# Gate and up projections of a gated mix as two by two blocks with seven products

## The chip, the cores and the metric

The kernel runs on one core of a Trainium2 chip. The metric is the device time of one execution in microseconds (us); the median of several runs is given.

## What is computed

With x of 2048 × 512, 32 heads of 16 and a hidden size F of 1792, the reference is

```
g = sigmoid((x * gate_w).sum(-1))
a = softmax_attention(x @ wqkv, 32 heads) @ wo
b = (sigmoid(x @ w_gate) * (x @ w_up)) @ w_down
out = g * a + (1 - g) * b
```

Every operand of a product is kept as a high and a low part, and a product is three matmuls: high by high, high by low, low by high.

## The kernel before

The order of the instructions on PE, ACT, DVE and POOL is the order in which the program emits them. SP only issues transfers; the framework orders those, and each waits at SP until its source is ready or its target is free, with all later ones behind it.

The work has three stages. First come q and k of the first 128 rows of weights and V for all tokens. Then 256 attention steps (the loop over k, NPER). Then the down projection in 28 chunks of 24 matmuls, with the heads' output projection between them.

A step handles two blocks of S (scores) for the row maxima, and two blocks of transposed S for the exponentials. The string STEADY is a step's order on PE: eight matmuls "m" (L257), each followed by a DVE reduction (L259) that reads the bank; eight matmuls "t" (L380), each followed by an exponential on ACT (L382); twelve half matmuls "d" (L145), of 64 rows each, of a dense sum into the bank dn; and a "turn" between d1, which uses the upper rows of PE, and d0, which uses the lower. The number behind m or t is the bank. A turn (L156) is a token on POOL: an empty instruction that waits for the last half before it and that the first half behind it waits for, so it also stands behind whatever POOL has to do ahead of it. After the step's order come 16 matmuls of exponentials by V, called values (L489), into the bank sm0 (SUMS = 0); they are copied out by ACT (L494) and summed on POOL (L506).

Dense sums are runs that the generator filling hands out: q and k of the remaining weights, then gate and up, one tile of 128 columns by 512 tokens each, 24 halves a run, so two steps. When a run is done, its bank is copied out (leave, L319, by ACT; by DVE, L308, in the last ten steps) and stored to gu_d or split for q_d and k_d. Work for POOL waits in the list later and is emitted by work(n), one piece at mid-step behind the turn, two at the end of a step. The maxima run LEAD = 20 blocks ahead, so the last ten steps (k = 246 on) have none: their banks come in turn from all seven others and DVE copies. The last eight steps (TAIL) follow the shorter order LAST with six d:

```
LAST = "t0 d1 t0 d1 t0 d1 turn t0 t1 t1 d0 t1 d0 t1 d0"
```

Dense work that is left then, ten runs, is done as whole matmuls of 128 rows (L582). Beside these runs ACT and DVE prepare the first chunks of the down stage: hidden (sigmoid on ACT, L453, product on DVE, L454) and hidden_split (copy to the high part on ACT, L94, subtraction on DVE, L97). The sigmoid isn't in ACT's table for exponentials, so ACT loads another table first. The down matmuls are L673.

Of the kernel before, what the change touches and what calls it, by code (L numbers as in the profile page):

```python
# [24 lines left out]
P = 128  # L25
KT = D // P
# [12 lines left out]
TAIL = 8  # L39
# [4 lines left out]
def gated_mix(ctx, tc, x, xT, wqk, wv, wo, w_gate, w_up, w_down, gate_w, out):  # L44
# [26 lines left out]
    rec_d = dram.tile([P, 512], F32, name="rec_d")  # L71
    max_d = dram.tile([2 * NPAIR, 4, 32, 2, 32], F32, name="max_d")
# [44 lines left out]
    def split_later(h, l, src, then=None):  # L117
# [4 lines left out]
        later.append(lambda: pool.tensor_copy(h, src))  # L122
        later.append(low)
# [37 lines left out]
    later = []  # L161

    def work(n):
        while later and n:
            later.pop(0)()
            n -= 1
# [11 lines left out]
    def load_x(c, raw=None, ks=range(KT)):  # L178
        raw = raw or mid(f"x{c}")
        cols = slice(c * 512, (c + 1) * 512)  # L180
        for k in ks:
            sp.dma_start(raw[:, k, :], xT[k * P:(k + 1) * P, cols])
# [85 lines left out]
    def put_max(half):  # L268
# [15 lines left out]
        return [lambda: pool.tensor_copy(hl[:, 0, :], mt), low]  # L284
# [3 lines left out]

    def filling():
        jobs = [("qk", c) for c in range(1, D // P)] + [("gu", f) for f in range(NF)] + [("down", 0)]  # L290

        def raws(kind, n):
            if kind == "qk":
                return [raw_cols(wqk, n, f"q{n}"), raw_cols(wqk, KT + n, f"k{n}")]
            if kind == "gu":
                return [raw_cols(w_gate, n, f"g{n}"), raw_cols(w_up, n, f"u{n}")]
            return [raw_weights(w_down[f * P:(f + 1) * P, :], [P, D], f"wd{f}") for f in range(2)]

        nxt = [split_weights(r) for r in raws(*jobs[0])]
        yield None  # L300
        for j, (kind, n) in enumerate(jobs[:-1]):
            ws, nxt = nxt, []
            for c in range(NC):
                for i, w in enumerate(ws):
                    run = Sum(bankd(), unit(w, c))
                    yield run
                    e = keep.tile([P, 512], F32, name=f"{kind}{n}_{c}_{i}", tag="er", bufs=4)
                    leave(e, run.o)  # L308
                    if kind == "qk":
                        put_qk(e, (q_d, k_d)[i], n, c)  # L310
                    else:
                        sp.dma_start(gu_d[i, n, :, c * 512:(c + 1) * 512], e)
                    if (c, i) == (0, 0):
                        coming = raws(*jobs[j + 1])
# [76 lines left out]
    for t in range(2, NS, 2):  # L391
        two = [Sum(bankv(), tokens(t + a)) for a in range(2)]
        for g in (LOW, UP):
# [13 lines left out]
            if t >= 12:  # L407
                work(1)
# [307 lines left out]
```

## Time and profile before

| | us |
|---|---|
| median of 3 runs | 1733.11 (1732.87 to 1733.24) |
| the profiled execution | 1733.32 |
| its span, first to last instruction | 1731.5 |
| values of step 0 to values of step 245 | 91.04 to 1459.92 |
| the last ten steps | 1459.92 to 1502.25 |
| the ten whole runs | 1502.25 to 1531.58 |
| the down stage | 1531.58 to 1731.5 |

Times in the profile count from the first instruction of the profiled execution; its own time is 1.82 us longer than its span. The granted clock of TensorE is 1.00 throughout. A line such as L489 is the line of the kernel before, and a shape such as 128x512 is partitions by elements. Rows of a timeline give start, length, engine, line, operation, output and input; the bracket at the end is the time for which the engine stood idle just before, and what ended that.

### The profile page before, as it was taken

To read this page: it belongs to the slowest core of one execution; us is meant where nothing else is said; L and a number is where in the kernel's file an instruction comes from. 1 tells how busy PE (TensorE), PEld (TensorE's weight loads), DVE (VectorE), ACT (ScalarE), POOL (GpSimd) and SP (SyncE) were. 2 spreads that over 40 slices of the span, in tenths; PEclk is the share of its full clock that TensorE was granted. 3 is DMA by queue.
4 is the path that set the end of the run, shared out by engine and by line. 5 is a ranking of instruction groups with operands and counts; after the bars stand their busy time and mean duration, and the time that the engine had idled before them with its cause. 6 is when DMAs were issued, how large, how long until landed. Compare 5 with 4: busy or idle time off the path is not lost.

```text
span 1731.5 us, 33713 instructions
## 1 busy us (share of the span) xinstructions
PE 1724.6 (100%) x12666; PEld 1066.3 (62%) x12666; DVE 1426.1 (82%) x2291; ACT 1319.3 (76%) x2555; POOL 471.0 (27%) x437
## 2 busy tenths in 40 slices
PE   9999999999999999999999999999999999999999
PEld 7755555555555555555555555555555555588887
DVE  6988888888999999998888888888888887457543
ACT  4188888888888888888888888888888888844321
POOL 1034343432222322222222222222222222343110
PEclk9999999999999999999999999999999999999999
DMA  9312424241314131314131313131221212377752
GB/s 252 80 43 68 83 68 93 69 107 43 81 57 81 57 81 40 82 50 87 38 75 39 75 39 64 44 63 51 53 57 46 56 55 69 118 233 257 237 194 73
DMA packets 85347, 149.78 MB, mean 86 GB/s; under 512 B 18816, under 2 KB 27008, under 8 KB 82304
## 3 DMA queue, kind: packets, MB, share of 16 engines
q1 hardware_dynamic: 85184, 147.63, 31.8%
q8 instruction: 99, 1.62, 0.4%
q14 instruction: 64, 0.52, 0.1%
HBM read 87.56 MB, written 60.03 MB: 85 GB/s over the span
## 4 chain that ended last, share of the span: by engine, by line
PE 97%; DVE 2%; DMA 0%; ACT 0%; issue 0%; SPq 0%; DVEq 0%
PE dn L145 29%; PE sm L489 27%; PE sm L257 12%; PE sm L673 7%; PE st L380 7%; PE sm L380 5%; PE st L132 3%; PE st L257 2%; DVE stat L259 2%; PE dn L673 2%; PE st L346 1%; PE sm L582 1%; PE st L582 1%; PE st L145 1%; PE st L489 0%; DMA x<-in_xT_dram 0%
## 5 line engine op out<-in xcount | busy, mean ns | idle before, releaser
L259 DVE TENSOR_REDUCE stat<-sm 128x1 f32<-128x512 f32 x1310 | 848.9, 684 | 154.8 <-PE sm L380 138.0
L382 ACT ACTIVATE p<-st 128x512 f32<-128x512 f32 x1019 | 612.8, 654 | 2.3 <-PE st L380 2.3
L382 ACT ACTIVATE p<-sm 128x512 f32<-128x512 f32 x1027 | 604.8, 630 | 2.4 <-PE sm L380 1.8
L257 PE MATMUL sm<-ks,qs 48*128 48x512 f32 x1310 | 521.0, 436 | 0.2
L506 POOL TENSOR_TENSOR sum<-sum,part 128x512 f32<-128x512 f32 x224 | 289.8, 1294 | 844.5 <-PE sm L380 779.1
L489 PE MATMUL sm<-p,v 128*17 128x512 f32 x4048 | 483.8, 595 | 0.0
L259 DVE TENSOR_REDUCE stat<-st 128x1 f32<-128x512 f32 x738 | 482.6, 682 | 0.1
L380 PE MATMUL sm<-qs,ks 64*128 64x512 f32 x1027 | 426.9, 421 | 0.8 <-ACT part L494 0.8
L380 PE MATMUL st<-qs,ks 64*128 64x512 f32 x1019 | 423.3, 419 | 0.0
L257 PEld LDWEIGHTS sm<-ks,qs 48*128 48x128 f32 x1310 | 238.0, 184 | 293.7 <-DVE stat L259 212.5
L257 PE MATMUL st<-ks,qs 48*128 48x512 f32 x738 | 291.4, 395 | 0.0
L494 ACT ACTIVATE part<-sm 128x512 f32<-128x512 f32 x215 | 128.7, 599 | 170.8 <-issue 146.9
L489 PEld LDWEIGHTS sm<-p,v 128*17 128x17 f32 x4048 | 93.7, 96 | 227.0 <-issue 159.3
L380 PEld LDWEIGHTS st<-qs,ks 64*128 64x128 f32 x1019 | 186.8, 184 | 28.7 <-issue 3.4
L380 PEld LDWEIGHTS sm<-qs,ks 64*128 64x128 f32 x1027 | 188.7, 185 | 12.7 <-issue 4.3
L257 PEld LDWEIGHTS st<-ks,qs 48*128 48x128 f32 x738 | 137.7, 187 | 1.1 <-ACT v L363 0.3
L454 DVE TENSOR_TENSOR gul<-gul 128x1024 f32<-128x1024 f32 (+1 forms) x30 | 47.2, 1579 | 33.8 <-ACT gul L453 31.1
L319 ACT ACTIVATE gu<-dn 128x512 f32<-128x512 f32 x99 | 68.8, 695 | 0.0
L673 PE MATMUL sm<-wd_h,hl 128*128 128x512 f32 x208 | 67.0, 389 | 0.0
L94 ACT ACTIVATE hl<-gul 128x1024 fp32r<-128x1024 f32 (+1 forms) x30 | 29.9, 998 | 41.4 <-PE sm L673 28.8
L94 ACT ACTIVATE oh<-ot 128x1024 fp32r<-128x1024 f32 x8 | 8.5, 1061 | 55.2 <-DVE ot L631 55.2
L97 POOL TENSOR_TENSOR ol<-ot,oh 128x1024 fp32r<-128x1024 f32 x8 | 19.3, 2410 | 109.5 <-ACT oh L94 99.1
(465 smaller groups left out, 2925.0 us busy)
## 6 DMA issues: line engine op xcount, KB each, us to landing
gu_d<-gu SPq DMA_DIRECT2D x112, 256.0 KB
gul<-gu_d SPq DMA_DIRECT2D x56, 512.0 KB
qs<-q_d SPq DMA_DIRECT2D x90, 128.0 KB
ks<-k_d SPq DMA_DIRECT2D x90, 128.0 KB
pv_d<-sum SPq DMA_DIRECT2D x32, 256.0 KB
q_d<-qe SPq DMA_DIRECT2D x12, 512.0 KB
k_d<-qe SPq DMA_DIRECT2D x12, 512.0 KB
x<-in_xT_dram SPq DMA_DIRECT2D x16, 256.0 KB
```

The source lines that it names most:

```text
L132: pe.matmul(o, a, b, start=(i == 0), stop=(i == len(ops) - 1))
L145: mm = pe.matmul(self.o, a[rows], b[rows], start=(self.n == 0), stop=(self.n == 2 * len(self.ops) - 1))
L257: pe.matmul(t, qs[r:r + KM, qt * P:(qt + 1) * P], ks[r:r + KM, g * 512:(g + 1) * 512], start=True, stop=True)
L259: dve.tensor_reduce(stat[half][:, b, qt % 8, g:g + 1], t, axis=AX.X, op=ALU.max)
L319: leave = lambda e, o: act.activation(e, o, AF.Copy)
L380: pe.matmul(o, ks[r:r + KR, (kt + a) * P:(kt + a + 1) * P], qs[r:r + KR, q0:q0 + 512], start=True, stop=True)
L382: act.activation(pt[:, 2 * a + c, :], o, AF.Exp, scale=DH ** -0.5)
L454: dve.tensor_tensor(gu[:, 1, a], gu[:, 0, a], gu[:, 1, a], ALU.mult)
L489: pe.matmul(o[32 * c:32 * c + VW, :], v[:, 2 * k % 16 + a, h * VW:(h + 1) * VW], pts[c // 2][:, 2 * a + c % 2, :], start=(a == 0), stop=(a ...
L494: act.activation(e, o, AF.Copy)
L506: pool.tensor_tensor(s, s, e, ALU.add)
L673: pe.matmul(down[t], a, b, start=(f == 0 and m == 0), stop=(f == NF - 2 and m == 5))
```

## The change

Gate and up are computed as two by two blocks: x in four blocks (tokens by half of the inner size), the weights in four blocks (half of the inner size by tile f or f + 7), and seven block products with sums of blocks in place of eight. The runs get a fourth of the old inner work each, 12 halves, so one step each, and come in three kinds of jobs: "far" (7 jobs of 4 runs, products without any sums of x), "side" (14 of 4) and "chain" (14 of 8).

The sums of blocks of x are made on POOL by mix_x after each of the first four far jobs (steps 52, 56, 60, 64), from blocks of x that are loaded again; one of them replaces a part of xh and xl at once, the others are split, stored to t_d and loaded into xh and xl later by mixed_x. The sums of weights are made on POOL too (op in weights). The products are added on POOL by plus, with earlier sums loaded back from gu_d, and stored. xT is laid out by the host in blocks of 128 × 512.

The lists of deferred work have costs now: work(1.3) at mid-step and work(2.6) at the end take pieces until their costs are used up, from later first and from slow (the mixes) after it; flush takes all.

All dense work lies in attention. Steps 0 to 238 are STEADY, 239 to 245 are BARE (no dense work, the free bank dn used as an eighth), 246 to 255 LAST. The ten whole runs are gone, and the down stage follows on attention at once. The first two chunks' sigmoids become hidden_early, emitted after the values of steps 250 and 252: exponential of −x on ACT, then on DVE plus one, a reciprocal of 128 × 1024 and the product; their splits are on DVE altogether. The values of step 255 and the second split stand inside chunk 0. The logits of g are spread over steps 78 to 125.

In the kernel after, L311 is the mix's subtraction, L127 and L124 are the two operations of split_later, L324 and L330 those of put_mix, L409 is the copy out of dn by DVE, L638 to L640 are hidden_early's, L681 is DVE's copy of the values, L266, L558 and L674 are S, transposed S and values on PE, and L150 is a dense half.

On POOL around step 56 the program before has the sums of values (part51 is that of step 51), the maxima's two small operations and a weight's split:

```order
L506 TENSOR_TENSOR sum3_0_4098<-sum3_0_4098,part50_4221 128x512
L506 TENSOR_TENSOR sum3_0_4098<-sum3_0_4098,part51_4282 128x512
L506 TENSOR_TENSOR sum3_0_4098<-sum3_0_4098,part52_4341 128x512
L284 CAST mhl3_1_4397<-mt3_1_4388 128x32
L275 TENSOR_TENSOR mhl3_1_4397<-mt3_1_4388,mhl3_1_4397 128x32
L506 TENSOR_TENSOR sum3_0_4098<-sum3_0_4098,part53_4413 128x512
L506 TENSOR_TENSOR sum3_0_4098<-sum3_0_4098,part54_4473 128x512
L122 CAST g1h_4526<-g1r_4150 128x512
```

In the program after, the end of the first mix (ml1_00 to ml2_00) and the start of the second (mix0_01) stand there:

```order
L324 CAST mh1_00_4512<-mix0_00_4287 128x512
L691 TENSOR_TENSOR sum3_0_4113<-sum3_0_4113,part54_4523 128x512
L330 TENSOR_TENSOR ml1_00_4576<-mix0_00_4287,mh1_00_4512 128x512
L324 CAST mh2_00_4579<-mix1_00_4288 128x512
L330 TENSOR_TENSOR ml2_00_4582<-mix1_00_4288,mh2_00_4579 128x512
L311 TENSOR_TENSOR mix0_01_4585<-mix0_01_4585 128x512
L127 CAST xh_106<-mix0_01_4585 128x512
L124 TENSOR_TENSOR xl_107<-mix0_01_4585,xh_106 128x512
L691 TENSOR_TENSOR sum3_0_4113<-sum3_0_4113,part55_4606 128x512
```

The subtraction of the second mix has come between the low half of the mix before and the sum of values of step 55, and each reads a tile that SP has to load.

On PE, this is a STEADY step before, from the fifth m, which is the second one of the step into sm0, to the last (qs1 and ks1 are the rows of the last pair of heads):

```order
L257 MATMUL sm0_69<-ks1_101,qs1_100 128x512
L380 MATMUL st0_65<-qs1_100,ks1_101 128x512
L257 MATMUL st1_66<-ks1_101,qs1_100 128x512
L145 MATMUL dn_68<-xh_105,g12h_15646 128x512
L145 MATMUL dn_68<-xl_106,g12h_15646 128x512
L380 MATMUL sm1_70<-qs1_100,ks1_101 128x512
L380 MATMUL st2_67<-qs1_100,ks1_101 128x512
L145 MATMUL dn_68<-xh_105,g12l_15647 128x512
L257 MATMUL sm2_71<-ks1_101,qs1_100 128x512
L145 MATMUL dn_68<-xh_105,g12h_15646 128x512
L257 MATMUL sm3_72<-ks1_101,qs1_100 128x512
L145 MATMUL dn_68<-xl_106,g12h_15646 128x512
```

And this is a BARE step after, from the first m into sm0 to the values of step 239:

```order
L266 MATMUL sm0_69<-ks1_102,qs1_101 128x512
L558 MATMUL st0_65<-qs0_99,ks0_100 128x512
L266 MATMUL dn_68<-ks1_102,qs1_101 128x512
L558 MATMUL st1_66<-qs1_101,ks1_102 128x512
L266 MATMUL sm2_71<-ks1_102,qs1_101 128x512
L558 MATMUL sm1_70<-qs1_101,ks1_102 128x512
L266 MATMUL sm0_69<-ks1_102,qs1_101 128x512
L558 MATMUL st2_67<-qs1_101,ks1_102 128x512
L266 MATMUL sm3_72<-ks1_102,qs1_101 128x512
L558 MATMUL st0_65<-qs1_101,ks1_102 128x512
L674 MATMUL sm0_69<-p239_1_17029,v_98 17x512 x2
```

The second m into sm0 was followed by three others in its step; it is now followed by one, and no dense half stands between.

On DVE, the copies of the last steps before are these (part250 is of step 250; den belongs to the heads):

```order
L496 COPY part250_16742<-sm2_71 128x512
L308 COPY gu12_2_0_16770<-dn_68 128x512
L496 COPY part251_16781<-st0_65 128x512
L465 RECIPROCAL den_93<-den_93 64x512
L496 COPY part252_16821<-st2_67 128x512
L496 COPY part253_16858<-sm1_70 128x512
L496 COPY part254_16895<-sm3_72 128x512
L308 COPY gu12_2_1_16914<-dn_68 128x512
```

After, they are:

```order
L681 COPY part249_17561<-st1_66 128x512
L681 COPY part250_17600<-st2_67 128x512
L638 TENSOR_SCALAR gul0_0_17519<-gul0_0_17519 128x1024
L639 RECIPROCAL gul0_0_17519<-gul0_0_17519 128x1024
L640 TENSOR_TENSOR gul0_0_17519<-gul0_0_17519 128x1024
L409 COPY chain16_11_17632<-dn_68 128x512
L681 COPY part251_17644<-sm3_72 128x512
L650 RECIPROCAL den_94<-den_94 64x512
L681 COPY part252_17687<-sm0_69 128x512
L638 TENSOR_SCALAR gul0_2_17522<-gul0_2_17522 128x1024
L639 RECIPROCAL gul0_2_17522<-gul0_2_17522 128x1024
L640 TENSOR_TENSOR gul0_2_17522<-gul0_2_17522 128x1024
```

The reciprocals of gul0_0 and gul0_2 and the operations beside them have come between the copy of a step's values and the next copy out of dn.

The diff, cut to its core:

```diff
-TAIL = 8
+FULL = 239
+FREE = NPER - LEAD // 2
+HF = NF // 2
...
-    later = []
-    def work(n):
-        while later and n:
-            later.pop(0)()
-            n -= 1
+    later, slow, soon = [], [], []
+    def work(length):
+        while length > 0.3 and (later or slow):
+            cost, step = (later or slow).pop(0)
+            step()
+            length -= cost
...
+    def mix_x(c, k):
+        one, two = [keep.tile([P, 2, 512], F32, name=f"mix{i}_{c}{k}", tag="ev", bufs=2) for i in range(2)]
+        for to, (ci, ki) in ((one[:, 0], (c + 2, k)), (one[:, 1], (c, k)), (two[:, 0], (c + 2, k + 2)), (two[:, 1], (c, k + 2))):
+            sp.dma_start(to, xT[ci, ki])
+        def minus(to, u, w):
+            slow.append((1.3, lambda: pool.tensor_tensor(to, u, w, ALU.subtract)))
+        minus(one[:, 1], one[:, 0], one[:, 1])
+        cols = slice((c + 2) * 512, (c + 3) * 512)
+        split_later(xh[:, k, cols], xl[:, k, cols], one[:, 1], queue=slow)
+        minus(one[:, 0], two[:, 0], one[:, 0])
+        minus(two[:, 0], two[:, 0], one[:, 1])
+        minus(two[:, 1], two[:, 1], two[:, 0])
+        for n, t in enumerate((two[:, 0], one[:, 0], two[:, 1])):
+            put_mix(n, c, k, t)
...
+        def low():
+            h = out.pop((n, c, k))
+            l = keep.tile([P, 512], F32R, name=f"ml{n}_{c}{k}", tag="er", bufs=4)
+            pool.tensor_tensor(l, t, h.bitcast(F32), ALU.subtract)
+            sp.dma_start(t_d[n, 1, c, k], l.bitcast(F32))
+        out = {}
+        slow.extend([(0.65, high), (1.3, low)])
...
+        pairs = [(m, i) for i in range(HF) for m in range(2)]
+        jobs = ([("qk", n) for n in range(1, D // P)] + [("far", i) for i in range(HF)]
+                + [("side", n) for n in pairs] + [("chain", n) for n in pairs] + [("down", 0)])
...
+            elif kind == "far":
+                for m in range(2):
+                    for c in range(2):
+                        run = Sum(bankd(), quarter(ws[m], 2, c))
+                        yield run
+                        sp.dma_start(place(m, n, c), out_of(run, f"far{m}{n}_{c}"))
+            elif kind == "side":
+                m, i = n
+                for c in range(2):
+                    for a in range(2):
+                        run = Sum(bankd(), quarter(ws[a], 2 * a, c + 2))
+                        yield run
+                        if n == pairs[-1]:
+                            mixed_x(1 + a, c, 2 * a, c + 2)
+                        e = out_of(run, f"side{m}{i}_{c}{a}")
+                        if a == 0:
+                            first = e
+                            sp.dma_start(place(m, i + HF, c + 2), e)
+                        else:
+                            plus(e, e, first, place(m, i, c + 2))
+            else:
+                m, i = n
+                for c in range(2):
+                    to = [place(m, i, c), place(m, i, c + 2), place(m, i + HF, c + 2), place(m, i + HF, c)]
+                    for a, (k0, cx) in enumerate(((0, c), (2, c), (0, c + 2), (2, c + 2))):
+                        if a in (0, 2):
+                            part = keep.tile([P, 2, 512], F32, name=f"had{m}{i}_{c}{a}", tag="ev", bufs=2)
+                        had = part[:, a % 2]
+                        if a < 3:
+                            sp.dma_start(had, to[a])
+                        run = Sum(bankd(), quarter(ws[a], k0, cx))
+                        yield run
+                        e = out_of(run, f"chain{m}{i}_{c}{a}")
+                        if a in (1, 2):
+                            plus(e, e, first)
+                        if a < 3:
+                            plus(had, e, had, to[a])
+                        else:
+                            plus(e, e, first, to[a])
+                        first = e
+        def plus(to, u, w, then=None):
+            def add():
+                pool.tensor_tensor(to, u, w, ALU.add)
+                if then is not None:
+                    sp.dma_start(then, to)
+            soon.append((1.3, add))
...
+            while end in later:
+                later.pop(0)[1]()
+            ws = new
+            if kind == "far" and n < 4:
+                flush(slow)
+                mix_x(n // 2, n % 2)
+            if kind == "far" and n == HF - 1:
+                flush(slow)
+                for c in range(2):
+                    mixed_x(0, c, 2, c)
...
+    eight = seven + [dn]
+    bank7 = turns([seven[b] for b in (5, 1, 6, 2, 3, 4, 0)])
...
+    def hidden_early(m):
+        gu = loaded[m]
+        act.activation(gu[:, 0], gu[:, 0], AF.Exp, scale=-1.0)
+        dve.tensor_scalar(gu[:, 0], gu[:, 0], 1.0, 3e38, op0=ALU.add, op1=ALU.min)
+        dve.reciprocal(gu[:, 0], gu[:, 0])
+        dve.tensor_tensor(gu[:, 1], gu[:, 0], gu[:, 1], ALU.mult)
+    def hidden_split(m, engine=act):
         hl = mid(f"hl{m}", F32R).rearrange("p (a f) s -> p a f s", a=2)
-        for a in (slice(0, 1), slice(1, 2)) if m < 2 else (slice(0, 2),):
-            split(hl[:, 0, a], hl[:, 1, a], loaded[m][:, 1, a], act, dve)
+        split(hl[:, 0], hl[:, 1], loaded[m][:, 1], engine, dve)
...
+    BARE = ("m1:7 t0:5 m1:2 t0:1 m1:3 t0:6 m1:0 t0:4 "
+            "m0:7 t1:5 m0:2 t1:1 m0:0 t1:6 m0:3 t1:4")
...
-        emit(STEADY if k < NPER - TAIL else LAST, **parts)
-        if k == NPER - 1:
-            bankd = bank
-        if run.done():
-            run = next(fill)
-        else:
+        emit(STEADY if k < FULL else BARE if k < FREE else LAST, **parts)
+        if run and run.done():
+            run = next(fill, None)
+        elif run and run.n:
...
-        work(2)
+        work(2.6)
+        later.extend(soon)
+        soon.clear()
...
+        if k in (NPER - 6, NPER - 4):
+            hidden_early((k - NPER + 6) // 2)
+    flush(later)
+    bank = turns(banks)
+    hidden_split(0, dve)
     act.activation(g1, logit, AF.Sigmoid)
     dve.tensor_scalar(g0, g1, -1.0, 1.0, op0=ALU.mult, op1=ALU.add)
-    values(NPER - 1)
-    work(len(later))
-    run = whole_run(run)
-    hidden(1)
-    hidden_split(1)
-    while run:
-        run = whole_run(run)
-        work(len(later))
...
+            if (n, t) == (0, 1):
+                values(NPER - 1)
+                flush(later)
+                hidden_split(1, dve)
```

More of the change, by code (lines that the diff above doesn't have):

```diff
@@ L294, in raws @@
                 return [raw_cols(wqk, n, f"q{n}"), raw_cols(wqk, KT + n, f"k{n}")]
[L295 to L299, printed above, removed]
-        yield None
[L301 to L310, printed above, removed]
-                    else:
-                        sp.dma_start(gu_d[i, n, :, c * 512:(c + 1) * 512], e)
-                    if (c, i) == (0, 0):
-                        coming = raws(*jobs[j + 1])
-                    if (c, i) in ((1, 1), (2, 1)):
-                        nxt.append(split_weights(coming[c - 1]))
@@ L317, in filling @@
-        wd.extend(nxt)
+            if kind == "far":
+                both = []
+                for m in range(2):
+                    raw = keep.tile([P, KT, P], F32, name=f"far{m}{n}r", tag="wr", bufs=2)
+                    sp.dma_start(raw[:, 2:], gu_w[m][n][:, 2:])
+                    both.append(raw)
+                return both
+            if kind == "down":
+                return [raw_weights(w_down[f * P:(f + 1) * P, :], [P, D], f"wd{f}") for f in range(2)]
+            m, i = n
@@ L502, in values @@
             put(e)
[L503 removed]
+            later.append((1.3, lambda s=sums[half]: add(s, e)))
         def add(s, e):
```

140 lines of the change are left out of this document (107 added, 33 removed).

## The prediction

> **What bounds the kernel now.** I read the page first: its span, its engines and the chain that ended last.
> ```profile
> span 1731.5 us, 33713 instructions
> PE 1724.6 (100%) x12666; PEld 1066.3 (62%) x12666; DVE 1426.1 (82%) x2291; ACT 1319.3 (76%) x2555; POOL 471.0 (27%) x437
> PE 97%; DVE 2%; DMA 0%; ACT 0%; issue 0%; SPq 0%; DVEq 0%
> ```
> PE looks like the bound everywhere. Its "busy" counts overlapping records, so a stretch needs its own look. The windows give busy time by stage (columns: PE, PEld, DVE, ACT, POOL, clock, DMA share, GB/s).
> ```profile
> 91.04:979.53 888.49, 888.49 (x6999) 513.91 (x6997) 793.32 (x1345) 757.03 (x1511) 270.90 (x267) 1.00 0.27 66
> 979.53:1459.92 480.39, 480.39 (x3786) 278.25 (x3785) 423.67 (x709) 409.51 (x818) 119.88 (x115) 1.00 0.24 58
> 1459.92:1502.25 42.33, 41.56 (x311) 19.11 (x309) 12.94 (x17) 38.78 (x80) 13.42 (x13) 1.00 0.12 40
> 1502.25:1531.58 29.33, 29.33 (x136) 22.86 (x137) 9.07 (x11) 12.18 (x21) 9.02 (x8) 1.00 0.76 255
> 1531.58:1570.00 38.42, 38.42 (x170) 31.51 (x169) 29.07 (x16) 22.88 (x25) 22.67 (x9) 1.00 0.82 277
> ```
> The edges are starts of values matmuls, so the first two windows hold 159 and 86 steps of the attention loop: 888.49/159 = 5.59 and 480.39/86 = 5.59 us a step, although POOL works 30% of the one and 25% of the other, and only every second step ends a dense sum. Something that is the same in all of them sets the pace. Then come the last ten steps, without row maxima (42.33), the ten whole dense runs (29.33) and the start of the down stage. One step, from values(244) to values(245), in the timelines of PE and, below it, of DVE:
> ```profile
> 1454.35 1.91 PE L489 MATMUL sm<-p,v 128*17 128x512 f32 x16
> 1456.19 0.49 PE L257 MATMUL sm<-ks,qs 48*128 48x512 f32 x1
> 1458.27 0.42 PE L145 MATMUL dn<-xh,g12h 64*128 64x512 f32 x1
> 1459.92 0.62 PE L489 MATMUL sm<-p,v 128*17 128x512 f32 x4
> 1456.72 0.69 DVE L259 TENSOR_REDUCE stat<-sm 128x1 f32<-128x512 f32 x1 [0.71 <-PE sm L380]
> 1457.33 1.28 DVE L259 TENSOR_REDUCE stat<-st 128x1 f32<-128x512 f32 x2
> 1458.53 1.28 DVE L259 TENSOR_REDUCE stat<-sm 128x1 f32<-128x512 f32 x2
> ```
> Maxima follow each other by 0.60 us (1456.72, 1457.33, ... 1458.53). The fifth, the second on bank sm0, ends at 1459.81, and 0.11 later the values matmuls enter sm0. So the step is a loop through DVE: 1.84 (values to the first S matmul, 1456.19) + 0.53 (to its reduction) + 4 × 0.60 (four more in turn) + 0.69 (the fifth's length) + 0.11 = 5.57. DVE is idle 0.71 a step, but only because the first S stands behind the values. Dense matmuls ride along in this loop. **Removing dense work inside attention therefore gains nothing there**; it gains what it empties behind attention. The other condition in the loop is d0: after the mid-step token it starts 3.92 after the values (1458.27), so POOL has until then to reach the token.
>
> **Part by part.** The profiled execution is 1733.32 (span + 1.82), 0.21 above the median of 1733.11; I add to 1733.32.
>
> *Fewer products.* 112 runs of 24 halves and the 24 of q/k become 24 of q/k and 196 of 12: 2928 dense halves, not 3264. Steps 0 to 238 stay STEADY at 5.59: 0 us. A run of 12 ends in every step, so ACT copies dn out in each, not in one of two: 0.35 us more a step on average for an ACT that is busy 409.51 of 480.39, 0.82 short of full: hidden, and steps with such a copy are no longer today. POOL gets 196 adds of products, up to two a step, their operands loaded a step ahead by SP. Rows with POOL's prices:
> ```profile
> L506 POOL TENSOR_TENSOR sum<-sum,part 128x512 f32<-128x512 f32 x139 | 179.5, 1291 | 478.7 <-PE sm L380 445.7 <-DMA pv_d<-sum 19.7 <-DMA gu_d<-gu 9.9
> L122 POOL CAST qe<-qk 128x512 fp32r<-128x512 f32 x24 | 14.6, 610 | 69.1 <-ACT qk L319 55.0 <-DMA ks<-k_d 7.4 <-PE sm L380 6.7
> ```
> A chain step has up to two adds (2.6), a share of the weights (three 128x256 operations, half of 1.29 each, and two splits of 0.61 + 1.29: 5.7 for 8 steps, 0.7) and the values sum (1.3): 4.6 of 5.59, hidden with 1.0 to spare. If that cover were gone, 112 steps would pay. The blocked xT, the logits' new steps and the reloads of the mixed x change no wait that I can find: 0 to −1 for the shorter first loads, left out.
>
> *Mixing x.* After far jobs 0 to 3 (steps 52, 56, 60, 64) POOL's first instruction is a subtraction of x blocks, put ahead of the mid-step token, and SP has the loads behind the store of that very step's leave. POOL's sequencer waits for them, the token behind it, d0 for the token, and PE's S and S^T behind d0. Step 60's loads stand ahead of that store, so three of four wait. The rows that price it:
> ```profile
> 1102.32 0.62 PE L489 MATMUL sm<-p,v 128*17 128x512 f32 x4
> 1103.81 0.32 SPq L312 DMA_DIRECT2D gu_d<-gu  x1
> 1105.20 0.32 SPq L277 DMA_DIRECT2D max_d<-mhl  x1
> 1106.65 2.78 SPq L281 DMA_DIRECT2D qs<-max_d  x4
> L421 SPq DMA_DIRECT2D gul<-gu_d x56: 359/430/856, 1424.7 to 1690.6; - x56
> ```
> A leave's store issues 1.49 after the values (1103.81 − 1102.32). The two loads that the subtraction needs follow at 0.43 each: issued by 2.4. A 32 KB transfer is waited on 1.45 after its issue (1105.20 to 1106.65), and 256 KB at 255 GB/s adds 1.0 (estimate): landing near 5.0. Then the subtraction 1.29, the CAST 0.61 and the dispatch of a third one: token at about 7.3 where 3.9 was due, 3.3 lost in step 52. In steps 56 and 64 the loads also await the tiles of the mix before, whose last two low halves and a CAST (2 × 1.29 + 0.61 = 3.2) POOL does at that same place: landing 7.4, token 9.5, 5.6 each. That is 14.5; some of it may issue earlier, and I take **+13**. Bounds: 0 (nothing waits) and 18 (all four).
>
> *Steps 239 to 245, BARE.* No dense work and eight banks, but values still go into sm0, and the second S in sm0 is now the seventh of eight, not the fifth. The loop is 1.84 + 0.53 + 6 × 0.60 + 0.69 + 0.11 = 6.76, seven times 1.18 more: **+8.3**. The other end is DVE alone, 8 × 0.60 = 4.78: −5.6. I take the first, since the order of PE fixes it.
>
> *Steps 246 to 255.* Maxima are over; steps 248 to 253 took (1498.26 − 1474.97)/6 = 3.88.
> ```profile
> 1474.97 0.62 PE L489 MATMUL st<-p,v 128*17 128x512 f32 x4
> 1498.26 2.00 PE L489 MATMUL sm<-p,v 128*17 128x512 f32 x16
> 1500.40 0.69 DVE L496 COPY part<-sm 128x512 f32<-128x512 f32 x1 [3.23 <-PE sm L489]
> L465 DVE RECIPROCAL den<-den x2: 3332/3340/3349, 1489.3 to 1587.3; 64x512 f32<-64x512 f32 x2
> L453 ACT ACTIVATE gul<-gul x30: 618/1046/1064, 1507.1 to 1697.9; 128x1024 f32<-128x1024 f32 x26, 128x512 f32<-128x512 f32 x4
> L454 DVE TENSOR_TENSOR gul<-gul x30: 686/1219/3421, 1507.8 to 1700.7; 128x1024 f32<-128x1024 f32 x26, 128x512 f32<-128x512 f32 x4
> ```
> All ten would take 39, not 42.33; two exponentials (1.05, as L453) on ACT, which paces these steps, make 41. A reciprocal of 512 columns takes 3.34, so 1024 take 6.7 (a row of 64 or of 128 partitions alike, I assume). After values(250) DVE copies its part at +2.1 (as 1500.40), then scalar op (1.1, between one and two 0.69 copies), reciprocal 6.7, product 1.2; only then, at 11.8, the leave of dn, 0.69. PE's first d1 of step 252 needs that bank: due at 3.88 + 1.84 + 1.05 = 6.8, it starts at 12.5 or later: 6 lost, and ACT starves behind PE. The second, two steps on, has den's reciprocal (3.34) ahead of it and loses 6 to 7. 41 + 13 = 54.3: **+12.0**. Bounds: −1 (hidden), +15.
>
> The Trainium skill ("VectorE: DVE Perf Modes", on SBUF-only operands) says that a scalar operation on fp32 from SBUF to SBUF reads two elements a clock, where one of two tensors can't; the scalar op would then take about 0.7 and both waits would shrink by 0.4. No row of this trace has one that large.
>
> *The tail.* Before, 29.4 of whole runs cover the first hidden blocks:
> ```profile
> 1502.18 0.51 PE L582 MATMUL sm<-xh,g12h 128*128 128x512 f32 x1
> 1505.84 1.28 ACT L453 ACT_TABLE_LOAD   x1
> 1531.58 0.39 PE L673 MATMUL sm<-wd0h,hl 128*128 128x512 f32 x1
> L97 DVE TENSOR_TENSOR hl<-gul,hl x30: 689/1218/3419, 1509.2 to 1712.3; 128x1024 fp32r<-128x1024 f32 x26, 128x512 fp32r<-128x512 f32 x4
> ```
> 170 matmuls took 38.42: 0.226 each, 5.4 a chunk of 24. Chunk 1 ended 29.3 + 10.8 = 40.2 after the last dense matmul. Now: leave 0.7, hl0's CAST up to 1.4 and subtraction 1.2, chunk 0 5.4 with values(255) 1.84 inside: 10.5. Chunk 1 needs hl1, whose CAST and subtraction stand on DVE behind the product of gul0_4; that tile's two loads of 512 KB wait for the last S^T: 0.43 + 1.45 + 2.06 (at 255 GB/s), about 4 and, the second behind it, 6 to 7. The table load (1.28) and the sigmoid hide in that; product 1.2, or 3.4 beside POOL, the copy of values(255) 0.7, CAST and subtraction 1.9 to 2.6: chunk 1 starts at 10.7 to 13.1 and ends at 16.1 to 18.5. That is 24.1 to 21.7 less: **−22.9**. Later chunks had DVE and the loads about at PE's pace, and get the same: 0.
>
> Sum: 13 + 8.3 + 12.0 − 22.9 = +10.4, 1743.7; rounded **1743.5 us**.
>
> **Rivals.**
> (a) *POOL's waits in the mixes are hidden*: SP's loads are issued early, as step 60's are. 1743.7 − 13 = 1730.7. For: POOL is idle 70%. Against: the store ahead of the loads waits for ACT.
> (b) *DVE's work finds its gaps*: BARE at 4.78 (−13.9) or the reciprocals hidden (−12), beside (a): 1730.7 − 13.9 = 1717, 1705 with both. This ends faster. The three stalls sum to 33.3 against a gain of 22.9, so it decides once over 10.4 of them are hidden. For: DVE is busy only 12.94 of 42.33 there. Against: both come from the order of one queue, not from its load.
> (c) *The clock.* All windows show 1.00, none with an idle PE. If stalls of 5.6 to 6.5 dropped it, four of them would each be followed by 3.4 us at half pace: 4 × 1.7 = 7, 1750. Beside it: the Trainium skill ("TensorE: Matmul & The Clock Gate", Part 1) says that an idle window of about 3.4 us halves the clock until as long a busy one; by that rule this happens, and no row here shows it.
> (d) *POOL becomes the bound of the chain*: at 4.6 of 5.59 a late token of 0.2 in 112 steps gives +22, 1766. Against: the token is not last in POOL's step.
> (e) The change doesn't do what it says: the halves are counted in the built program, so under 1%.
>
> **How the numbers follow.** Forecast 0.50 (its own range 1737 to 1753); (a) 0.16; (b) 0.21; (c) 0.07; (d) and like 0.06. About 0.2%, 3.5 us, is what a measurement of this kernel can tell from no change: 1729.6 to 1736.6. Faster: (b) and 0.07 of (a), 0.28. Within: 0.09 of (a) and 0.03 of the forecast, 0.12. Slower: 0.60. The range leaves out half of (b) and (d): 1714 to 1756.
>
> **What would show it.** Right: waits of PE for POOL's token in steps 52, 56 and 64 only, of 3 and 5 to 6 us; BARE steps at 6.7; in steps 252 and 254 PE idle behind a DVE leave; the first down matmul 3 to 4 us after the last dense one, the second chunk's 11 to 13 after. Wrong: BARE under 5.6, no reciprocal ahead of a leave, or steps in the chain over 5.6, which would put POOL in the loop.

## The result and the profile after

| | before | after |
|---|---|---|
| median, us | 1732.99 (4 runs) | 1783.18 (4 runs, 1778.36 to 1784.94) |
| ratio | | 1.0286, 95% interval 1.0273 to 1.0298 |
| span of the profiled execution | 1731.5 | 1783.2 |

The forecast was slower, and it is slower, but by 50 us and not by 10. The page of the kernel after, with the row of the granted clock in 40 slices and the chain:

```profile
span 1783.2 us, 34285 instructions
PE 1721.3 (97%) x12450; PEld 1040.4 (58%) x12450; DVE 1434.0 (80%) x2295; ACT 1357.2 (76%) x2631; POOL 873.2 (49%) x849
PEclk9999999999899999999999999999999997899999
PE 88%; DVE 3%; DMA 3%; ACT 1%; issue 1%; POOL 1%; SPq 1%; POOLq 0%; DVEq 0%; ACTq 0%
```

PE has 216 matmuls fewer and is busy 3 us less, in a span that is 52 us longer: it now waits. Before, the chain was PE for 97%; now DVE, DMA, ACT, POOL and SP are on it. And the clock row isn't all nines any more.

The windows, first of the kernel after, then of the one before, with the same edges in the work: the values of steps 51, 70, 238, 245 and 254, the first matmul of the third chunk, the end. (Columns: length; PE, PEld, DVE, ACT, POOL; clock; DMA share; GB/s.)

```profile
375.54:506.65 131.11, 115.75 (x838) 64.50 (x836) 94.15 (x159) 95.83 (x191) 83.50 (x91) 0.91 0.51 158
506.65:1446.39 939.74, 939.74 (x7394) 542.85 (x7392) 837.91 (x1419) 841.72 (x1681) 577.22 (x571) 1.00 0.43 120
1446.39:1499.00 52.61, 40.63 (x226) 13.67 (x224) 35.24 (x59) 33.81 (x66) 14.91 (x13) 0.84 0.23 71
1499.00:1553.57 54.57, 42.08 (x270) 18.25 (x271) 29.46 (x22) 37.02 (x74) 17.10 (x15) 0.81 0.11 35
1553.57:1577.17 23.60, 20.40 (x92) 12.18 (x91) 13.67 (x11) 11.24 (x18) 14.35 (x9) 0.85 0.67 216
1577.17:1783.16 205.99, 189.52 (x817) 154.81 (x815) 100.79 (x90) 61.18 (x62) 37.32 (x14) 0.96 0.59 192
```

```profile
375.86:481.87 106.01, 106.01 (x839) 61.41 (x837) 95.16 (x163) 90.69 (x182) 27.02 (x27) 1.00 0.27 67
481.87:1420.86 938.99, 938.99 (x7395) 543.25 (x7393) 836.80 (x1415) 800.11 (x1597) 240.02 (x233) 1.00 0.24 59
1420.86:1459.92 39.06, 39.06 (x310) 22.72 (x309) 34.12 (x57) 33.06 (x67) 7.74 (x6) 1.00 0.25 82
1459.92:1498.26 38.34, 37.57 (x284) 17.45 (x282) 12.25 (x16) 34.79 (x71) 12.06 (x12) 1.00 0.13 44
1498.26:1542.76 44.50, 44.50 (x212) 33.46 (x211) 18.36 (x17) 24.94 (x41) 19.13 (x14) 1.00 0.64 211
1542.76:1731.55 188.79, 185.12 (x817) 153.02 (x815) 106.48 (x89) 60.32 (x60) 36.54 (x14) 1.00 0.60 198
```

Row by row the difference is +25.1 (the mixes), +0.8 (168 steps with seven products), +13.6 (BARE), +16.2 (last steps), −20.9 (tail) and +17.2 (the rest of the down stage); with −0.3 ahead of them that is the 51.6. Every row but the second has a clock below 1.00 after, and all had 1.00 before. What PE waited for in the whole run (us in total, number of waits, longest):

```profile
PE dn L150 <- POOLq L161: 15.4, 3, 6.0
PE dn L150 <- DVE chain L409: 11.9, 2, 6.2
PE dn L850 <- DVE hl L100: 10.6, 2, 9.6
PE sm L674 <- DVE stat L268: 6.8, 7, 1.1
PE sm L266 <- DVE stat L268: 4.8, 7, 0.7
```

Five lines: the token behind the mixes, the copy of dn behind the reciprocals, one hidden block of the down stage, and the two of BARE. Together they are 49.5. That this is near 51.6 is chance: the tail also gained 20.9, so far more was lost than these waits.

One of the mixes, in step 52, in timelines of SP, POOL and PE. The values of step 51 start at 375.54:

```profile
377.01 0.32 SPq L428 DMA_DIRECT2D gu_d<-far  x1
377.38 1.87 SPq L308 DMA_DIRECT2D mix<-in_xT_dram  x4
381.78 1.26 POOL L311 TENSOR_TENSOR mix<-mix 128x512 f32<-128x512 f32 x1 [6.53 <-DMA mix<-in_xT_dram]
383.83 0.79 PE L150 MATMUL dn<-xh,far01h 64*128 64x512 f32 x1 [3.83 <-POOLq L161]
```

The store issues 1.47 behind the values, the four loads right behind it, POOL waits for them until 6.24, and PE stands idle for 3.83 ahead of its first d0.

The first reciprocal, DVE and then PE, with two pairs of dense matmuls, one right behind the stall and one later:

```profile
1525.06 6.55 DVE L639 RECIPROCAL gul<-gul 128x1024 f32<-128x1024 f32 x1
1532.79 0.68 DVE L409 COPY chain<-dn 128x512 f32<-128x512 f32 x1
1533.52 0.79 PE L150 MATMUL dn<-xh,ca(1, 6)h 64*128 64x512 f32 x1 [6.21 <-DVE chain L409]
1534.12 0.62 PE L150 MATMUL dn<-xl,ca(1, 6)h 64*128 64x512 f32 x1
1534.54 0.62 PE L150 MATMUL dn<-xh,ca(1, 6)l 64*128 64x512 f32 x1
1540.54 0.39 PE L150 MATMUL dn<-xl,ca(1, 6)h 64*128 64x512 f32 x1
1540.78 0.39 PE L150 MATMUL dn<-xh,ca(1, 6)l 64*128 64x512 f32 x1
```

The stall is where the prediction put it. But behind it two matmuls follow each other by 0.42 us, where 0.24 us is usual. The granted clock there is 0.50, from 1529.70 to 1539.94.

The long wait of the down stage, with SP's issue of the second denominators' load after and, last, before:

```profile
1639.60 0.73 SPq L649 DMA_DIRECT2D den<-pv_d  x1
1647.21 3.35 DVE L650 RECIPROCAL den<-den 64x512 f32<-64x512 f32 x1 [15.11 <-DMA den<-pv_d]
1653.01 1.22 PE L850 MATMUL dn<-wd_h,hl 128*128 128x512 f32 x2 [9.57 <-DVE hl L100]
```

```profile
1519.28 0.47 SPq L464 DMA_DIRECT2D den<-pv_d  x1
```

Before, this load went out 12 us ahead of the down stage. After, it goes out 81 us into it, and DVE, whose order is fixed, stands still for it with the next hidden block behind. Its source, the last sum of values, was stored at 1513.05 before and is stored at 1570.94 after, since values(255) now stand in chunk 0; so 69 of the 81 us are the place in SP's queue.

### The profile page after: what moved, and what is told of

It is laid out like the page before. It is cut to its first block, busy times and chain, and to the rows that moved or that the text cites. A ratio compares the mean times of both kernels' runs of the same rounds, so it can differ in the third digit from the quotient of the medians.

```text
span 1783.2 us, 34285 instructions
## 1 busy us (share of the span) xinstructions
PE 1721.3 (97%) x12450; PEld 1040.4 (58%) x12450; DVE 1434.0 (80%) x2295; ACT 1357.2 (76%) x2631; POOL 873.2 (49%) x849
## 4 chain that ended last, share of the span: by engine, by line
PE 88%; DVE 3%; DMA 3%; ACT 1%; issue 1%; POOL 1%; SPq 1%; POOLq 0%; DVEq 0%; ACTq 0%
PE dn L150 27%; PE sm L674 26%; PE sm L266 12%; PE st L558 6%; PE sm L850 4%; PE sm L558 4%; PE st L266 2%; PE st L137 2%; DVE stat L268 2%; PE st L150 1%; PE dn L850 1%; DMA gul<-gu_d 1%; PE st L524 1%; ACT p L560 1%; DVE gul L639 1%
## 5 line engine op out<-in xcount | busy, mean ns | idle before, releaser
L560 ACT ACTIVATE p<-st 128x512 f32<-128x512 f32 x1034 | 620.7, 645 | 4.0 <-PE st L558 3.7
L266 PE MATMUL sm<-ks,qs 48*128 48x512 f32 x1317 | 524.8, 439 | 5.3 <-DVE stat L268 4.8
L674 PE MATMUL sm<-p,v 128*17 128x512 f32 x4032 | 494.2, 608 | 6.8 <-DVE stat L268 6.8
L268 DVE TENSOR_REDUCE stat<-st 128x1 f32<-128x512 f32 x717 | 467.7, 680 | 0.2 <-PE st L266 0.2
L558 PE MATMUL st<-qs,ks 64*128 64x512 f32 x1034 | 436.3, 425 | 0.0
L558 PE MATMUL sm<-qs,ks 64*128 64x512 f32 x1012 | 426.7, 424 | 0.6 <-ACT p L560 0.6
L266 PEld LDWEIGHTS sm<-ks,qs 48*128 48x128 f32 x1317 | 240.5, 185 | 298.9 <-DVE stat L268 215.9
L266 PE MATMUL st<-ks,qs 48*128 48x512 f32 x717 | 283.1, 395 | 0.0
L674 PEld LDWEIGHTS sm<-p,v 128*17 128x17 f32 x4032 | 94.5, 98 | 242.6 <-issue 163.4
L558 PEld LDWEIGHTS st<-qs,ks 64*128 64x128 f32 x1034 | 192.4, 187 | 30.9 <-issue 5.7
L558 PEld LDWEIGHTS sm<-qs,ks 64*128 64x128 f32 x1012 | 188.2, 187 | 11.4 <-issue 4.3
L466 POOL TENSOR_TENSOR had<-chain,had 128x512 f32<-128x512 f32 x84 | 108.0, 1285 | 64.3 <-PE sm L558 36.1
L266 PEld LDWEIGHTS st<-ks,qs 48*128 48x128 f32 x717 | 133.8, 187 | 1.4 <-ACT v L541 0.3
L466 POOL TENSOR_TENSOR chain<-chain,chain 128x512 f32<-128x512 f32 x84 | 108.6, 1293 | 23.0 <-PE st L558 11.7
L466 POOL TENSOR_TENSOR side<-side,side 128x512 f32<-128x512 f32 x28 | 36.2, 1291 | 79.6 <-PE sm L558 74.2
L497 ACT ACTIVATE chain<-dn 128x512 f32<-128x512 f32 x107 | 73.7, 689 | 0.0
```

The costliest lines, as they stand in the source:

```text
L266: pe.matmul(t, qs[r:r + KM, qt * P:(qt + 1) * P], ks[r:r + KM, g * 512:(g + 1) * 512], start=True, stop=True)
L268: dve.tensor_reduce(stat[half][:, b, qt % 8, g:g + 1], t, axis=AX.X, op=ALU.max)
L466: pool.tensor_tensor(to, u, w, ALU.add)
L497: leave = lambda e, o: act.activation(e, o, AF.Copy)
L558: pe.matmul(o, ks[r:r + KR, (kt + a) * P:(kt + a + 1) * P], qs[r:r + KR, q0:q0 + 512], start=True, stop=True)
L560: act.activation(pt[:, 2 * a + c, :], o, AF.Exp, scale=DH ** -0.5)
```

## The experiments

The theory after the result: (A) each stall stands where the trace names it, and (B) a stalled or partly idle PE loses its clock and pays a second time. The rivals are named run by run; the stages are those of the windows above.

### The mixes' work, later

```diff
+    wait = [0]
     def work(length):
-        while length > 0.3 and (later or slow):
+        length = max(length, 2.6) if slow and not wait[0] else length
+        while length > 0.3 and (later or slow and not wait[0]):
...
+        wait[0] = max(0, wait[0] - 1)
...
             slow.append((1.3, lambda: pool.tensor_tensor(to, u, w, ALU.subtract)))
+        wait[0] = 2
```

> The mixes' POOL work starts two calls of work later, when the x blocks have landed; nothing else is changed. Theory A (the loads that SP issues in that step make POOL, the token and PE wait, and each such wait is followed by some us at half clock): steps 52, 56 and 64 go back to 5.6 us and the steps behind them too, 25 us less than the changed kernel. Rival (POOL's own work of the mixes, some 13 us in four steps, makes the token late wherever it stands): the waits move to other steps of the far phase and at most 8 us are won.

1769.35 us (1764.38 to 1771.23), 13.8 less than the changed kernel. The stage of the mixes, and PE's waits in it:

```profile
375.95:489.45 113.50, 110.18 (x839) 62.95 (x837) 94.38 (x159) 96.13 (x191) 83.32 (x91) 0.98 0.59 183
PE dn L150 <- ACT far L502: 2.0, 1, 2.0
PE dn L150 <- POOLq L161: 1.3, 3, 0.8
```

POOL does the same work, 83.3 us, and 17.6 of the 25.1 are gone: it was the loads. (The edit also lets a call at mid-step take 2.6 us of the mixes' work, where it took 1.3; POOL's share is the same.) The 7.5 left are a wait for ACT's copy out of dn, short ones for the token, and the steps behind them. The kernel as a whole gained less than the stage, since its BARE steps had the low clock in six of seven (58.0 for 52.6), of which below.

### The second denominators, loaded early

```diff
+    def denominators_load(i):
...
                 values(NPER - 1)
                 flush(later)
+                denominators_load(1)
```

> Only the load of the second half of the denominators is issued earlier, behind values(255), where before it stood in SP's queue behind loads and stores of the down stage; the reciprocal stays where it is on DVE. Theory A (DVE's reciprocal waits 15 us for a load that stands late in SP's queue, and the hidden block behind it on DVE comes 9.6 us late to PE): 11 to 13 us less than the changed kernel, the 9.6 and the slow clock behind it. Rival (the down stage lacks DMA bandwidth, since the whole runs no longer cover its loads): the wait moves to the next chunk's loads and at most 3 us are won.

1775.70 us, 7.5 less. The four times are 1767.67, 1770.81, 1780.59 and 1781.51; the profiled execution is the first, so its stages say more than the median. BARE and the down stage in it:

```profile
1445.78:1492.72 46.94, 34.21 (x227) 12.25 (x225) 35.26 (x59) 33.25 (x66) 14.86 (x13) 1.00 0.25 79
1569.27:1765.89 196.62, 188.35 (x817) 153.64 (x815) 103.51 (x90) 61.57 (x63) 37.00 (x14) 0.99 0.61 201
```

The down stage loses 9.4 of its 17.2: the wait of 9.6 is gone and none has taken its place. That is less than the 11 to 13 expected; waits of 1.1 to 1.4 are left. The first row is a windfall: here BARE kept its clock, and its seven steps took 6.71 each, 7.9 in all above before.

### Sigmoids in place of the early reciprocals

```diff
-        if k in (NPER - 6, NPER - 4):
-            hidden_early((k - NPER + 6) // 2)
...
+    hidden(0)
     hidden_split(0, dve)
+    hidden(1)
```

> The two early sigmoids (exponential, plus one, reciprocal) are undone: sigmoids on ACT and the products right behind attention, all else as in the changed kernel. Theory A (the reciprocals stand on DVE ahead of the copy out of dn, and PE stalls twice): steps 246 to 255 take 42 us and not 58, the tail up to its second chunk 4 us more: 12 us less than the changed kernel. Rival (the reciprocals cost no more than table load, sigmoids and products in the open): within 3 us of the changed kernel.

1751.27 us (1748.18 to 1756.69), 31.9 less, far more than the 12 expected. The last steps and the down stage:

```profile
1499.26:1535.74 36.48, 36.48 (x271) 16.07 (x271) 12.51 (x16) 33.22 (x68) 16.53 (x15) 0.95 0.16 53
1561.66:1752.16 190.50, 185.55 (x817) 152.81 (x815) 103.75 (x90) 60.61 (x61) 36.48 (x14) 1.00 0.62 205
```

54.57 becomes 36.48, 18.1 less, and the tail grows by 2.3: theory A, with the clock on top (0.81 becomes 0.95). The other 15.5 come from the down stage, which this edit doesn't touch: the framework orders SP anew for every program, and here put the denominators' load at 1588, not at 1640 as in the changed kernel.

### STEADY's order in the steps without dense work

```diff
-    BARE = ("m1:7 t0:5 m1:2 t0:1 m1:3 t0:6 m1:0 t0:4 "
-            "m0:7 t1:5 m0:2 t1:1 m0:0 t1:6 m0:3 t1:4")
+    BARE = ("m1:3 t0:2 m0:4 t0:5 m0:6 t0:1 m0:3 t0:2 m0:0 t1:4 "
+            "m1:5 t1:1 t1:6 m1:2 m1:3 t1:4")
```

> Steps 239 to 245 without dense work keep STEADY's order and banks of the maxima, so sm0's second one is the fifth again. Theory A (order alone makes these steps long): all seven take 5.6 us, 13 less than the changed kernel. Theory B (an idle PE loses its clock and the slow matmuls make the last three of them long): the loop of 6.7 becomes 5.6 in the first steps but the clock falls within the seven steps again and some of them stay near 7: 5 to 9 us less. If neither order nor clock matters: no change.

1769.41 us (1768.38 to 1771.66), 13.8 less:

```profile
1448.50:1487.54 39.04, 39.04 (x227) 20.36 (x225) 34.12 (x57) 32.09 (x65) 14.94 (x13) 1.00 0.31 95
```

All 13.6 are gone, with the same 227 matmuls, and the clock stays at 1.00. That is theory A's number and not B's 5 to 9: at 5.58 a step PE is busy throughout and keeps its clock. But order alone isn't worth 13.6. With the BARE order and full clock the seven steps cost 7.9 (the run above with the denominators), so the other 5.7 are the clock that the longer loop lost.

### BARE with a busier PE

```diff
+                for _ in range(again[0]):
...
+        again[0] = 3 if FULL <= k < FREE else 1
```

> Steps 239 to 245 keep their order and banks, but each transposed S is computed three times over into the same bank, so PE has 16 matmuls more in each of these steps and idles less; nothing waits for more. Theory B (PE's idle share in these steps lets the clock fall, and with it the last ones take 8.4 to 8.7): all seven take 6.7, granted clock 1.00 there, some 5 us less than the changed kernel. Rival (the order makes them 8.7 by itself, or the clock falls by a rule of its own): steps of 8.4 to 8.7 stay, or all become longer by the added matmuls.

1779.26 us (1779.07 to 1779.47), 3.9 less, with 111 matmuls more:

```profile
1445.35:1494.82 49.47, 49.36 (x338) 31.32 (x337) 36.46 (x59) 36.59 (x65) 14.96 (x13) 1.00 0.23 76
```

All seven steps take 7.07, none 8.4 or 8.7, at a clock of 1.00. The added matmuls cost 0.36 a step and win more than that. The four runs lie within 0.4 us, those of the changed kernel within 6.6. That the clock in these steps made that spread is likely and not shown. In the profiled executions with steps of 6.71 it was low in three, six, four and one of the seven (the changed kernel, the first run here, the one with sigmoids, the one with pieces below) and in none of the run with the early denominators. What decides that stays open.

### The reciprocals in pieces

```diff
+        part = gu[:, 0, q // 2, q % 2 * 256:q % 2 * 256 + 256]
+        dve.reciprocal(part, part)
-        dve.reciprocal(gu[:, 0], gu[:, 0])
...
-        if n == NSTEP - 16:
+        if n == NSTEP - 30:
             loaded.extend(hidden_load(*chunks[m]) for m in range(2))
-        if n == NSTEP - 10:
-            denominators(0)
...
-        if k in (NPER - 6, NPER - 4):
-            hidden_early((k - NPER + 6) // 2)
+        if NPER - 10 <= k < NPER - 2:
+            hidden_early(*divmod(k - NPER + 10, 4))
...
+        if n == 1:
+            denominators(0)
```

> The early sigmoids stay, but their reciprocals come in eight pieces of 256 columns, one behind each of values(246) to values(253), and their loads seven steps earlier; the first reciprocal of the denominators goes behind chunk 1. Theory A (the price is where the reciprocals stand on DVE, as one piece of 6.6 us ahead of the copy out of dn): a piece of 1.7 fits DVE's idle time of a step, steps 246 to 255 take 41 to 43 us where the changed kernel takes 58, and the kernel 15 to 17 less. Rival (DVE has not the time for them in these steps): pieces and copies still end late, and at most half of that is won.

1769.52 us (1766.59 to 1776.98), 13.7 less:

```profile
1495.22:1534.11 38.89, 37.94 (x271) 16.53 (x271) 25.63 (x26) 34.99 (x70) 17.02 (x15) 0.96 0.14 46
```

54.57 becomes 38.89, about before's 38.34, with the same reciprocals of the hidden blocks, now eight of 1.74: DVE has the time, and the price was the place. The first reciprocal of the denominators has left these steps too, but in the changed kernel nothing waited for it: it ended at 1537.32, and DVE then stood idle for 3.13. (PE's wait for dn is gone; the down stage keeps its late denominators, 207.6.)

### No dense work left for the last steps

```diff
-                turn(run)
+                if run and run.n:
+                    turn(run)
...
-        emit(STEADY if k < FULL else BARE if k < FREE else LAST, **parts)
+        emit(STEADY if k < FREE else LAST, **parts)
```

> Dense work goes on in STEADY until it is used up (step 243), so no BARE order and no dense work or copy out of dn in steps 246 to 255; the early reciprocals stay as they are. Theory A1 (the reciprocals cost because the copy out of dn stands behind them): with that copy gone steps 246 to 255 take about 42 us and not 58, and steps 239 to 245 39 and not 53: 29 us less than the changed kernel. Rival A2 (any copy behind them does it: the values' copy is next, and its bank comes round again within nine matmuls): the stall moves to the transposed S that needs the values' bank, steps 246 to 255 still take 52 to 58 us, and only 12 to 14 us are won.

1750.31 us (1748.75 to 1754.17), 32.9 less. The last steps, and one of the stalls in them:

```profile
1483.47:1532.28 48.81, 37.48 (x218) 14.81 (x217) 27.84 (x20) 38.39 (x76) 10.75 (x10) 0.92 0.09 26
1516.84 0.79 PE L558 MATMUL sm<-qs,ks 64*128 64x512 f32 x1 [5.04 <-DVE part L681]
```

A2 has the mechanism: without a copy out of dn PE waits for the values' copy behind the same reciprocal, 5.0 in place of 6.2, and 10.5 above before remain. The 33 won come from BARE (13.6), from here (5.8) and, again, from another order on SP (down stage 191.7, denominators' load at 1584). That the whole comes near A1's 29 is chance.

### Stalls of chosen length

In the kernel before, POOL multiplies ahead of the token of six steps:

```diff
+    pool.memset(den, 1.0)
...
+    delay = {60: 4, 75: 5, 90: 6, 105: 7, 125: 8, 139: 10}
...
+        for _ in range(delay.get(k, 0)):
+            pool.tensor_tensor(den, den, den, ALU.mult)
```

> The kernel before, with extra multiplications of 1.29 us on POOL ahead of the token of six steps: 4 in step 60, 5 in 75, 6 in 90, 7 in 105, 8 in 125, 10 in 139. The token's slack is about 4.2 us, so PE is stalled for about 1, 2.3, 3.6, 4.8, 6.1 and 8.7 us. Theory B (a long idle time of PE halves its clock for a time behind it): a stall below some length costs its own length, a longer one also makes the step behind it longer by 1.5 to 2 us, whatever its length. Rival (what made the steps behind the mixes longer was the mixes' work and transfers): each stall costs its own length, and the granted clock stays 1.00.

One run, 1755.77 us. Three of PE's waits, and the windows of the two steps from each:

```profile
680.69 0.79 PE L146 MATMUL dn<-xh,g3h 64*128 64x512 f32 x1 [2.58 <-POOLq L157]
799.33 0.67 PE L146 MATMUL dn<-xh,g4h 64*128 64x512 f32 x1 [3.67 <-POOLq L157]
885.38 0.79 PE L146 MATMUL dn<-xh,u5h 64*128 64x512 f32 x1 [5.90 <-POOLq L157]
673.67:690.74 17.07, 14.49 (x91) 7.39 (x89) 9.85 (x17) 9.74 (x20) 8.57 (x8) 0.80 0.08 32
791.20:808.04 16.84, 13.17 (x91) 7.18 (x89) 10.28 (x19) 9.71 (x20) 11.30 (x12) 0.90 0.09 32
875.02:895.70 20.68, 14.78 (x90) 7.33 (x88) 10.06 (x17) 9.80 (x20) 14.75 (x14) 0.75 0.10 27
```

A multiplication took 1.04 and not 1.29, so the stalls are shorter than planned, and step 90 had none. Two steps are 11.16, so waits of 2.58, 3.67 and 5.90 cost 5.9, 5.7 and 9.5: 3.3, 2.0 and 3.6 more than themselves. The short ones, 0.5 in step 60 and 0.6 at a weight load in step 75, cost 1.0 and 1.1, with no slow step behind. So theory B holds in kind, with no mix in the program, but the price is larger than its 1.5 to 2, and it doesn't grow in step with the wait.

The granted clock shows what is paid. It is 0.50 from 680.03 to 686.86, from 799.49 to 802.90 and from 881.41 to 891.65, and PE works 6.17, 3.41 and 6.27 us in these stretches. Half of that, 3.1, 1.7 and 3.1, is about the price. In all traces of this case half clock lasts 3.41 us or two, three or four times that; only the piece at a trace's end differs.

### All repairs together

The four edits of the first four runs at once, and then the same with the reciprocals in pieces and not the sigmoids.

> Four repairs at once: the mixes' work started later, STEADY's order of the maxima in the steps without dense work, sigmoids in place of the early reciprocals, and the second denominators' load issued earlier. If the parts add (read from the stages of their own runs: 7 left of the mixes' 25, 0 of 13, 40 and not 58 in the last steps, 22 to the second chunk, 190.5 behind it), the span is about 1721 and the kernel 10 us faster than the one before. Rival (the down stage now lacks the loads that 29 us of whole runs covered, so what is won ahead of it is given back in it): no faster than the one before, 1730 or more.

1724.25 us (1721.77 to 1728.06, 5 runs), ratio to the kernel before 0.9946, interval 0.9934 to 0.9959: faster by half a per cent. Mixes, steps 239 to 245, tail and down stage:

```profile
375.66:488.00 112.34, 108.43 (x838) 61.66 (x837) 94.22 (x159) 95.58 (x191) 83.39 (x91) 1.00 0.58 185
1427.52:1466.54 39.02, 39.02 (x227) 20.35 (x225) 34.14 (x57) 32.09 (x65) 14.90 (x13) 1.00 0.29 96
1503.33:1529.05 25.72, 20.08 (x92) 12.38 (x91) 14.04 (x14) 14.62 (x23) 12.85 (x10) 0.87 0.67 223
1529.05:1719.98 190.93, 185.77 (x817) 152.81 (x815) 103.61 (x90) 61.80 (x62) 37.17 (x15) 1.00 0.63 204
```

The parts add: a span of 1720.0 where 1721 was expected, in the profiled execution, which is the fastest of the five (the median's span is 1722.5). The scheme is worth 9 us here; what it gains, 18.8 in the tail, is partly eaten by the 6.3 left in the mixes and 2.1 in the down stage.

> The same four repairs, but with the reciprocals in pieces and not the sigmoids: two us less in the tail than with sigmoids if the pieces hide, 1718 to 1720 in all. Rival: the down stage waits for its loads and gives it back, 1730 or more.

1729.74 us (1727.90 to 1732.06, 11 runs), ratio 0.9981 (0.9972 to 0.9990): 5.5 slower than with sigmoids, not two faster.

```profile
1505.67:1529.67 24.00, 20.08 (x92) 12.22 (x91) 17.54 (x14) 12.48 (x21) 14.55 (x10) 0.86 0.67 213
1529.67:1727.34 197.67, 189.95 (x817) 154.37 (x815) 108.11 (x91) 61.43 (x63) 38.44 (x14) 0.98 0.61 201
```

The tail is 1.7 shorter, and the down stage 6.7 longer: its hidden blocks wait for their loads (DVE waits 32.0 us for gul between 1510 and 1640, with sigmoids 11.6). The order of SP is another one here too, the first two hidden blocks are loaded earlier, and the first reciprocal of the denominators stands behind chunk 1. Which of these does it wasn't tried.

## Why the prediction was wrong

**Right:** what sets the step, that seven products gain nothing inside attention and cost nothing there (0.8 in 168 steps), the steps and the mechanism of all three groups of stalls, and the waits themselves: 15.4 for the token in three steps (14.5 worked out, 13 taken), 11.9 for dn in steps 252 and 254 (12 to 13), 6.71 for a BARE step (6.76). The tail gave 20.9 (22.9), though two of its signs were off: the first down matmul started 1.9 behind the last dense one (3 to 4), the second chunk's 14.0 (11 to 13). One sum is off by a little: 41 + 13 is 54.0 and not 54.3.

Measured and forecast are 41 us apart in the profiled execution: 12.1 in the mixes, 5.3 in BARE, 4.2 in the last steps, 2.0 in the tail and 17.2 in the rest of the down stage.

**The step that failed first** is the one that priced each stall at its own length and left the clock to a rival with 0.07. The mixes cost 25.1 with waits of 15.4, BARE 13.6 with a longer loop worth 7.9, the last steps 16.2 and not 12.0: by subtraction, some 20 us of slow clock. PE worked 46 us at half clock in these three stages, which is 23 us lost at most. Rival (c) had the mechanism, but with 1.7 us for each of four stalls; the probe showed 2.0 to 3.6, and BARE has no stall over 1.1 us at all, and could lose its clock by being idle a quarter of the time (busy 40.63 of 52.61). The prediction should have carried this as a term of the sum: it had four stalls of 5.6 to 6.5 us in hand, one of 3.3, and no row of an idle PE in the trace, and a rule of the Trainium skill ("TensorE: Matmul & The Clock Gate", Part 1) that said what happens then. The trace now agrees with that rule in its main point, half the clock after an idle time of microseconds. It differs in the threshold: 2.58 us of waiting were enough. That a PE which idles in pieces can lose its clock too is what BARE shows.

**The second** is the sentence that later chunks "get the same: 0". It looked at DVE and at bandwidth, not at the order on SP. Before, SP had issued 12 loads of hidden blocks when it came to the second denominators' load; after, it had issued 28, and twelve of the heads' loads and two stores of the result. This order is fixed when the program is built, so it could have been compared ahead of any run. Early issue alone won 9.4 of the 17.2; orders of SP in which it happens to be early (with sigmoids, or without dense work in the end) gave 190.5 and 191.7 for 188.8. The rest of the 17.2, and why the framework moves that load so far, stay open.

The range, 1714 to 1756, was built from waits hidden or not; it had no case in which three stages pay for the clock and the down stage grows as well.

## What to carry to other kernels

A change that trades matmuls for waits must be priced with the clock: here a stall of 2.6 to 5.9 us cost 2.0 to 3.6 more than its length, and a PE that idled a quarter of its time lost its clock in four of five programs. Prefer an order that keeps it fed. A long instruction on an in-order engine costs by what stands behind it, so cut it into pieces that fit the idle time, and ask what is next behind it before removing the first victim. Where a scheduler orders a queue, compare that queue's whole order, also in stages that the edit doesn't touch.

## What the runs showed of the hardware that was not expected

- After a wait of 2.58, 3.67 or 5.90 us PE's next step or two ran slow: matmuls 0.42 apart and not 0.23, 2.0 to 3.6 us lost. Half clock came in pieces of 3.41 us: two, one and three of them. After a wait of 0.5 us no slow step followed.
- PE with 227 matmuls in seven steps of 6.71 lost its clock in none, one, three, four or six of these steps in different programs; with 338 in seven of 7.07, or 227 in seven of 5.58, in none.
- Adding 111 matmuls that write the same result again made the kernel 3.9 us faster and its runs agree within 0.4 us.
- A reciprocal of 1024 columns by 128 partitions took 6.55 us, of 512 columns by 64 partitions 3.33: 6.4 to 6.5 ns a column, with 128 rows and with 64.
- DVE's scalar operation on 128x1024 from SBUF to SBUF took 0.68 us, and 1.15 the other time; the product of two such tensors 1.22. The two elements a clock of the Trainium skill ("VectorE: DVE Perf Modes", Mode 2×_2P, on SBUF-only operands) agree with the 0.68. Why the other one took 1.15 is open.
